# Loads that cast on their way into double-buffered bf16 tiles, in place of casts and spreads on Pool, and a last token tile in column halves

## The chip, the cores and the metric

One core of one Trainium2 chip. The metric is the device time of one execution in microseconds (us), taken as the median of several executions. A profile is one execution with every instruction recorded; its span is some 1.7 us shorter than the time of the same execution (325.9 for 327.63 in before). The engines are TensorE (PE, with its weight loads PEld), VectorE (DVE), ScalarE (ACT), Pool (POOL, GpSimd) and SyncE (SP). "L289" is a line of the kernel whose profile is shown; the changed kernel's lines are a few further down (L289 of before is L298 of after, 295 is 304, 411 is 420, 412 is 421, 454 is 463).

## The reference, cut to what matters

```python
def _attn_ref(q, k, v):                     # (8 batches, 8 heads, 576, 64), f32
    scores = matmul(q, k.T) / sqrt(64)
    mask_local   = (rel >= 0) & (rel < 32)                        # heads 0 to 3
    mask_strided = (rel >= 0) & (pos[None] % 32 == pos[:, None] % 32)   # heads 4 to 7
    attn = softmax(where(mask, scores, -1e9))
    return attn @ v

def _moe_ref(x, w_in, w_out):               # x (4608, 512), w_in (512, 2048), w_out (2048, 512)
    h = x @ w_in
    g = where(h > 0, h, exp(min(h, 0)) - 1) # ELU
    return g @ w_out
```

The two matrix products of the second part are most of TensorE's work. The attention of batches 3 to 7 is woven between them, one batch in about 33 us.

## The kernel before

q, k and v of the local heads are loaded in f32 for most batches, and cast by Pool into one bf16 tile each. Strided v (`vs`) is loaded in bf16 and *spread* by Pool, that is, copied into a tile that holds columns of ones between the heads, so that one matmul gives both the products and the sums of the softmax.

```python
    ql32 = const([RS, HG, NS * D], F32, "ql32")      # f32, one buffer each
    kl32 = const([LQ, 2, 2, LB, D], F32, "kl32")
    vl32 = const([128, 2, 2, LB, D], F32, "vl32")
    qlb = const([RP, 2, NS, 2 * D], BF16, "qlb")     # bf16, one buffer each
    klb = const([LQ, 2, LB, 2 * D], BF16, "klb")
    vlx = [const([128, 2, LB, 3 * D], BF16, f"vlx{i}") for i in range(2)]   # v, ones, v
    vsx = [const([RS, 2, NS, 3 * D], BF16, f"vsx{i}") for i in range(2)]
    # ... cut ...
    for b in range(3, B):                            # places in the schedule of batch b
        st = int(SC[b][0])
        ld, sp, ca, tr = (9, 3, 5, 3) if b == 3 else (9, 6, 5, 3)
        if b > 3:
            at(st - ld, lambda b=b: (load_str(b, qs, q), load_str(b, ks, k), load_str(b, vs, v),
                                     load_kl(b, nc.gpsimd), load_ql(b, nc.gpsimd),
                                     load_vl(b, nc.gpsimd)))
        at(st - sp, lambda b=b: spreads(b))          # 2 copies on Pool
        for i, f in enumerate(casts(b)):             # 2 casts each of k, q and v on Pool
            at(st - ca + .5 * i, f)
        at(st - tr, lambda b=b: Ts(b))               # 4 transposes by DMA
```

The mask multiplies and the ELU on VectorE:

```python
            nc.vector.tensor_mul(pm..., e..., mask_s...)          # L289, two SBUF inputs
            nc.vector.tensor_mul(pm, e, mb...)                    # L295, two SBUF inputs
    # ... cut; the ELU of one group of the first product ...
            eng.tensor_scalar(e1, e, scalar1=1.0, scalar2=1.0,    # L411, one SBUF input
                              op0=ALU.min, op1=ALU.subtract)
            nc.vector.tensor_tensor(gt, e1, hps, op=ALU.max)      # L412, hps is in PSUM
    # ... cut; the end of a tile of the second product ...
            nc.scalar.copy(o_sb, ops)                             # L459
            store(j * SUB + kk * 128, o_sb)
```

The softmax here doesn't subtract the row's maximum and nothing guards it: scores larger than these inputs give would overflow.

Of the kernel before, what the change touches and what calls it, by code (L numbers as in the profile page):

```python
# [17 lines left out]
D = 64  # L18
HG = 4
# [11 lines left out]
def kernel(  # L31
# [37 lines left out]

    ql32 = const([RS, HG, NS * D], F32, "ql32")  # L70
    kl32 = const([LQ, 2, 2, LB, D], F32, "kl32")
# [3 lines left out]
    vs = const([RS, HG, NS * D], BF16, "vs")  # L75
    qlb = const([RP, 2, NS, 2 * D], BF16, "qlb")
    qld = qlb.rearrange("p a s c -> p (a s c)").rearrange("p (h c) -> p h c", h=HG)
    klb = const([LQ, 2, LB, 2 * D], BF16, "klb")

    KLW = PRE + 2 * S  # L80
    KSW = 16 * RP + 48
# [30 lines left out]
    def load_ql16(b):  # L112
        nc.gpsimd.dma_start(out=qld[0:RS], in_=q[b, 0:HG].rearrange("h (p s) d -> p h (s d)", s=NS))

    def load_kl16(b):
        for h in range(HG):
            nc.gpsimd.dma_start(
                out=klb[:, h // 2, :, (h % 2) * D:(h % 2 + 1) * D],
                in_=k[b, h].rearrange("(t p) d -> p t d", p=LQ))

    def load_vl16(b):
        for h in range(HG):
# [3 lines left out]
            nc.gpsimd.dma_start(out=t[0:PRE, 1:], in_=x[LQ - PRE:, 0:LB - 1, :])  # L126

    def load_str(b, dst, src):
        nc.gpsimd.dma_start(  # L129
            out=dst[0:RS], in_=src[b, HG:2 * HG].rearrange("h (p s) d -> p h (s d)", s=NS))  # L130

    def cast_q(eng, a):
        o = qlb[0:RS, a].rearrange("p s (x d) -> p s x d", x=2)
        i = ql32[:, 2 * a:2 * a + 2].rearrange("p x (s d) -> p s x d", d=D)
        (eng.copy if eng is nc.scalar else eng.tensor_copy)(o, i)  # L135

    def cast_k(eng, a):
        (eng.copy if eng is nc.scalar else eng.tensor_copy)(  # L138
            klb[:, a].rearrange("p t (x d) -> p t x d", x=2),
            kl32[:, a].rearrange("p x t d -> p t x d"))  # L140
# [5 lines left out]

    def spread_v(eng, b, a):
        o = vsx[b % 2][:, a].rearrange("p s (y d) -> p s y d", d=D)[:, :, 0:3:2, :]
        i = vs[:, 2 * a:2 * a + 2].rearrange("p x (s d) -> p s x d", d=D)
        (eng.copy if eng is nc.scalar else eng.tensor_copy)(o, i)  # L150

    def dma_T(b, which):
        i = b % 2
        out_, in_, n = {
            "qs": (qsT[i], qs.rearrange("p h c -> p (h c)"), RP),
            "ks": (ksT[i][:, 0:16 * RP], ks.rearrange("p h c -> p (h c)"), RP),
            "ql": (qlT[i], qlb.rearrange("p a s c -> p (a s c)"), RP),
            "kl": (klT[i][:, PRE:], klb.rearrange("p a t c -> p (a t c)"), LQ),
        }[which]
        nc.sync.dma_start_transpose(out=out_.rearrange("p (c n) -> p c n", n=n), in_=in_)  # L160
# [30 lines left out]
    nc.gpsimd.iota(dist, pattern=[[1, RS]], base=RS, channel_multiplier=-1)  # L191
    nc.vector.memset(qlb[64:RP], 0.0)
    load_vl(0, nc.gpsimd)
# [33 lines left out]
    def t_parts(b, hp, nm):  # L227
# [5 lines left out]
        elif nm == "q":  # L233
            dst = qlT[i][:, a * 8 * n:(a + 1) * 8 * n]
            blk = ([qlb[0:n, a, j] for j in range(NS)] if b not in (1, 2) else
                   [[qld[0:n, 2 * a + x, j * D:(j + 1) * D] for x in range(2)]
                    for j in range(NS)])
        else:
            dst = klT[i][:, PRE + a * S:PRE + (a + 1) * S]
            blk = [klb[:, a, j] for j in range(LB)]  # L240
        return dst, blk
# [172 lines left out]
    def l1_wide(j, t):  # L414
# [5 lines left out]
        for mm in range(4):  # L420
            for c in range(KC):
# [4 lines left out]
                    start=(c == 0), stop=(c == KC - 1))  # L426
        e = p_wide.tile([128, 4, SUB], F32, tag="we", name="we")
        nc.scalar.activation(e, hps, ACT.Exp)
# [6 lines left out]

    def store(c0, o_sb):
        c = c0
        while c < c0 + 128:
            b, r = divmod(c, S)
            s, p = divmod(r, RS)  # L440
            n = min(RS - p, c0 + 128 - c)
            nc.sync.dma_start(out=out_v[b, s, p:p + n, :],
                              in_=o_sb[c - c0:c - c0 + n, :])
            c += n

    acc = {}

    def l2(j, kk, part, pool, tag):
# [8 lines left out]
        if part == 3:  # L457
            o_sb = p_wk.tile([128, d_model], F32, tag="osb", name="osb")
            nc.scalar.copy(o_sb, ops)  # L459
            store(j * SUB + kk * 128, o_sb)  # L460


# [70 lines left out]

    def casts(b):
        return ([lambda a=a: cast_k(nc.gpsimd, a) for a in range(2)]
                + [lambda a=a: cast_q(nc.gpsimd, a) for a in range(2)]
                + [lambda a=a: cast_v(nc.gpsimd, b, a) for a in range(2)])

    def spreads(b):
        for a in range(2):  # L540
            spread_v(nc.gpsimd, b, a)

    one_columns(1)
# [10 lines left out]
    load_wo(3)  # L554
    load_kl(1, nc.gpsimd)
    load_ql16(1)
    load_vl(1, nc.gpsimd)

# [8 lines left out]
    load_str(2, qs, q)  # L567
    load_str(2, ks, k)


# [3 lines left out]
    def l2_to(n):  # L574
        while l2n[0] < min(n, len(L2S)):
            j, kk, part = L2S[l2n[0]]
            late = kk and j == NSUB - 1
            l2(j, kk, part, *((p_h, "h") if late else (p_o, "o")))
            l2n[0] += 1

    for it in ("2 S4 2 S5 2 2 B4 S6 2 E4 A5 S7 2 E5 B6 a 2 E6 A7 2 E7 v "
               "T0 2 S0 S1 c 2 T1 k B0 2 E0 S2 2 A1 E1 S3 2 B2 E2 2 A3 2 E3 t 2 x").split():
        n = int(it[-1]) if it[-1].isdigit() else 0
        if it == "2":
            l2_to(l2n[0] + 1)
        elif it == "v":
            load_str(2, vs, v)
            load_vl16(2)
        elif it == "a":
            cast_k(nc.gpsimd, 0)  # L590
            for a in range(2):
                cast_v(nc.gpsimd, 1, a)
        elif it == "c":
            cast_k(nc.scalar, 1)
        elif it == "k":
            load_kl16(2)
            load_ql16(2)
            load_kl(3, nc.gpsimd)
            load_ql(3, nc.gpsimd)
            load_vl(3, nc.gpsimd)  # L600
        elif it == "t":
            for p in (2, 3):
                piece_T(2, p)
        elif it == "x":
            load_str(3, qs, q)
            load_str(3, ks, k)
        elif it[0] == "T":
            piece_T(1, n, (nc.vector, nc.scalar))
# [20 lines left out]
    for b in range(3, B):  # L629
        st = int(SC[b][0])  # L630
        ld, sp, ca, tr = (9, 3, 5, 3) if b == 3 else (9, 6, 5, 3)
        if b > 3:
            at(st - ld, lambda b=b: (load_str(b, qs, q), load_str(b, ks, k), load_str(b, vs, v),
                                     load_kl(b, nc.gpsimd), load_ql(b, nc.gpsimd),
                                     load_vl(b, nc.gpsimd)))
        at(st - sp, lambda b=b: spreads(b))
        for i, f in enumerate(casts(b)):
            at(st - ca + .5 * i, f)
        at(st - tr, lambda b=b: Ts(b))
    for b in range(2, B):  # L640
# [5 lines left out]

    at(SC[2][1] + 2, lambda: load_str(3, vs, v))
    L1S = [(j, t) for j in range(2, NSUB) for t in range(8)]
# [38 lines left out]
```

## Time and profile before

| | before |
|---|---|
| time before the change was run, median of 3 | 328.34 us (327.12 to 328.93) |
| profiled span | 325.9 us |
| last matmul ends | 4.1 us before the end |
| Pool's instructions that compute, per batch from 3 on | 8, about 8 us |

The prediction shows the page's shares and the stretches. Beside them I use two more views. The first is the page: its count of DMA packets, and groups of instructions (line, engine, operation, output and inputs, shapes, count, then busy us and mean ns of one, then idle time before them and what ended it).

```profile
DMA packets 55179, 41.98 MB, mean 129 GB/s; under 512 B 38296, under 2 KB 45784, under 8 KB 55144
...
L411 DVE TENSOR_SCALAR he<-he 128x512 bf16<-128x512 f32 x130 | 59.9, 461 | 20.5 <-ACT he L404 19.1
...
L295 DVE TENSOR_TENSOR pm<-e,mask_l 128x576 bf16<-128x576 bf16 x32 | 17.9, 591 | 3.3 <-ACT e L287 3.0
L150 POOL COPY vsx<-vs 72x1024 bf16<-72x1024 bf16 x10 | 11.2, 1146 | 23.9 <-DMA vs<-in_v_dram 18.8
```

The busy time of a group counts overlapping instructions once, so 17.9 us over 32 is 0.56 us each, a little under the mean of one.

The second view is TensorE's timeline (start in us, length of one, line, operation, tiles, shapes, count; in brackets the wait before it and what ended it).

```profile
31.25 1.03 PE L397 MATMUL hps<-xT,w_in_sb 128*128 128x256 bf16 x8 [0.39 <-DVE g L412]
...
120.45 0.30 PE L284 MATMUL sc<-qlT,klT 64*128 64x96 bf16 x6 [0.77 <-DVE xT L308]
...
218.85 0.30 PE L284 MATMUL sc<-qlT,klT 64*128 64x96 bf16 x6 [0.56 <-DVE xT L308]
```

The last two are gaps of the attention of batches 3 to 7: TensorE stands still while VectorE finishes.

### The profile page before, as it was taken

What the parts mean: (1) busy time and instruction counts of PE and PEld (TensorE: products, weight loads), DVE (VectorE), ACT (ScalarE), POOL (GpSimd) and SP (SyncE); (2) the same over time, 40 slices, a digit from 0 to 9 for tenths busy, and PEclk for the clock granted to TensorE, in tenths of its full rate; (3) what the DMA queues carried; (4) which work ended last, traced back from release to release, by engine and by line L of the source; (5) the groups of instructions that cost most, each with busy time, mean ns of one, the idle gap of its engine ahead of it and who ended that gap; (6) DMA issues with size and microseconds to landing.
All of it is one profiled execution on the core that took longest, in us unless ns stands there. A gap on an engine that the chain in (4) does not pass through costs nothing.

```text
span 325.9 us, 7664 instructions
## 1 busy us (share of the span) xinstructions
PE 309.4 (95%) x2933; PEld 222.6 (68%) x2976; DVE 246.0 (75%) x481; ACT 221.0 (68%) x429; POOL 101.2 (31%) x121
## 2 busy tenths in 40 slices
PE   8899997989999989999999999989999999999994
PEld 6669944566667767767777677757777777777762
DVE  6764973467778898898888988998888866666660
ACT  3798765687778877777778777877877734444431
POOL 6262414962672445263245443540000000000000
PEclk9999999999999999999999999999999999999999
DMA  8999999999799939992999299939111111111212
GB/s 165 192 207 209 221 185 151 141 193 184 114 126 214 202 87 146 224 183 68 132 224 217 70 144 232 174 92 162 48 45 37 34 34 32 33 34 44 55 32 64
DMA packets 55179, 41.98 MB, mean 129 GB/s; under 512 B 38296, under 2 KB 45784, under 8 KB 55144
## 3 DMA queue, kind: packets, MB, share of 16 engines
q0 software_dynamic: 21040, 24.49, 45.7%
q1 hardware_dynamic: 32780, 16.42, 24.6%
q10 hardware_dynamic: 1324, 0.59, 0.8%
q8 instruction: 23, 0.38, 0.5%
q14 instruction: 12, 0.10, 0.1%
HBM read 38.18 MB, written 9.44 MB: 146 GB/s over the span
## 4 chain that ended last, share of the span: by engine, by line
PE 74%; DVE 13%; ACT 5%; issue 4%; DMA 3%; POOL 0%; DVEq 0%; ACTq 0%
PE ops L454 32%; PE hps L397 30%; DVE g L412 3%; PE ox L336 3%; PE sc L284 3%; DVE he L411 3%; DMA ks<-in_k_dram 3%; DVE xT L304 2%; PE idle L464 1%; DVE pm L295 1%; DVE g L431 1%; PE hpw L422 1%; DVE xT L308 1%; PE tp L261 1%; PE o_ps L369 1%
## 5 line engine op out<-in xcount | busy, mean ns | idle before, releaser
L454 PE MATMUL ops<-w_out_sb,g 128*128 128x512 bf16 x533 | 140.5, 380 | 2.7 <-issue 0.8
L397 PE MATMUL hps<-xT,w_in_sb 128*128 128x256 bf16 x1088 | 140.7, 273 | 0.6 <-DVE g L412 0.4
L397 PEld LDWEIGHTS <-w_in_sb 128*128 128x128 bf16 x1088 | 117.4, 114 | 22.7 <-issue 0.6
L404 ACT ACTIVATE he<-hps 128x512 f32<-128x512 f32 x136 | 80.2, 593 | 53.7 <-PE hps L397 52.7
L412 DVE TENSOR_TENSOR g<-he,hps 128x512 bf16<-128x512 bf16 x130 | 89.4, 687 | 13.5
L454 PEld LDWEIGHTS <-g 128*128 128x128 bf16 x576 | 52.0, 98 | 39.1 <-DVE g L412 0.3
L411 DVE TENSOR_SCALAR he<-he 128x512 bf16<-128x512 f32 x130 | 59.9, 461 | 20.5 <-ACT he L404 19.1
L287 ACT ACTIVATE e<-sc 128x576 bf16<-128x576 f32 (+1 forms) x64 | 38.6, 645 | 4.5 <-PE sc L284 4.4
L459 ACT COPY osb<-ops 128x512 f32<-128x512 f32 x36 | 21.1, 587 | 15.5 <-PE ops L454 13.2
L339 ACT ACTIVATE ln<-ox 64x288 f32<-64x288 f32 x40 | 16.3, 409 | 12.3 <-PE ox L336 11.7
L304 DVE TENSOR_TENSOR xT<-ox,rc 64x288 bf16<-64x288 f32 x40 | 18.1, 453 | 5.0 <-ACT rc L342 4.7
L308 DVE TENSOR_TENSOR xT<-ox,rc 64x288 bf16<-64x288 f32 x40 | 18.1, 453 | 4.0 <-ACT rc L342 3.7
L295 DVE TENSOR_TENSOR pm<-e,mask_l 128x576 bf16<-128x576 bf16 x32 | 17.9, 591 | 3.3 <-ACT e L287 3.0
L150 POOL COPY vsx<-vs 72x1024 bf16<-72x1024 bf16 x10 | 11.2, 1146 | 23.9 <-DMA vs<-in_v_dram 18.8
L342 ACT ACTIVATE rc<-ln 128x288 f32<-128x288 f32 x40 | 17.7, 443 | 1.3
L289 DVE TENSOR_TENSOR pm<-e,mask_s 72x576 bf16<-72x576 bf16 x32 | 16.0, 527 | 2.5 <-ACT e L287 2.2
L340 ACT ACTIVATE ln<-ox 64x288 f32<-64x288 f32 x40 | 16.1, 402 | 0.5
L464 PE MATMUL idle<-warm 128*128 128x256 bf16 x92 | 15.1, 312 | 1.3 <-DVE warm L173 1.3
L144 POOL CAST vlx<-vl 128x768 bf16<-128x768 f32 x13 | 10.6, 843 | 17.6 <-DMA vl<-in_v_dram 16.6
L138 POOL CAST klb<-kl 96x768 bf16<-96x768 f32 x11 | 9.8, 907 | 19.9 <-DMA kl<-in_k_dram 14.8
L129 POOL DMA_DIRECT2D qs<-in_q_dram x8 | 6.5, 806 | 29.9 <-DMA qsT<-qs 25.2
L135 POOL CAST qlb<-ql 72x1024 bf16<-72x1024 f32 x10 | 11.6, 1186 | 3.8 <-DMA ql<-in_q_dram 3.8
(98 smaller groups left out, 256.4 us busy)
## 6 DMA issues: line engine op xcount, KB each, us to landing
out_dram<-osb SPq DMA_DIRECT2D x32, 144.0 KB
vl<-in_v_dram POOLq DMA_DIRECT2D x7, 576.0 KB, 17.8
kl<-in_k_dram POOLq DMA_DIRECT2D x6, 576.0 KB, 14.6
ql<-in_q_dram POOLq DMA_DIRECT2D x5, 576.0 KB, 15.7
qs<-in_q_dram POOLq DMA_DIRECT2D x8, 288.0 KB, 7.4
ks<-in_k_dram POOLq DMA_DIRECT2D x8, 288.0 KB, 9.7
vs<-in_v_dram POOLq DMA_DIRECT2D x8, 288.0 KB, 9.7
w_in_sb<-in_moe_w_in_dram POOLq DMA_DIRECT2D x2, 1024.0 KB, 16.3
```

The lines of the kernel that those rows point to most:

```text
L287: nc.scalar.activation(e[0:R], sc[0:R, :, 0:W], ACT.Exp, scale=scale)
L295: nc.vector.tensor_mul(pm, e, mb.unsqueeze(1).to_broadcast([128, 2, W]))
L304: nc.vector.tensor_mul(xs[:, u * W:(u + 1) * W], o[pr], rc[pr])
L308: nc.vector.tensor_mul(dst, o[pr].rearrange(pat, b=3, s=NS), rc[pr].rearrange(pat, b=3, s=NS))
L342: nc.scalar.activation(rc, ln, ACT.Exp, scale=-1.0)
L397: nc.tensor.matmul(hps[:, mm], lhsT=w_in_of(m, c), rhs=xT[:, c, r0:r0 + SUB], start=(c == 0), stop=(c == KC - 1))
L404: nc.scalar.activation(e, hps, ACT.Exp)
L411: eng.tensor_scalar(e1, e, scalar1=1.0, scalar2=1.0, op0=ALU.min, op1=ALU.subtract)
L412: nc.vector.tensor_tensor(gt, e1, hps, op=ALU.max)
L454: nc.tensor.matmul(ops, lhsT=g[:, m, kk * 128:(kk + 1) * 128], rhs=w_out_sb[:, m, :], start=(m == 0), stop=(m == MC - 1))
L459: nc.scalar.copy(o_sb, ops)
L464: nc.tensor.matmul(ps, lhsT=warm[:, 0:128], rhs=warm[:, 0:ps.shape[-1]], start=True, stop=True, skip_group_check=True)
```

## The change

The intent: let the loads cast, so that Pool computes nothing after the start and VectorE gets its shared memory port back. The targets need two buffers, since a load now writes straight into what the transposes read. (The space comes from one f32 tile, `big`, that batch 0's q and the wide exponentials of the start now share.) At the end, the last tile of the output is computed in two column halves, so that the first half is copied and stored while TensorE does the second.

```diff
-    qlb = const([RP, 2, NS, 2 * D], BF16, "qlb")
-    klb = const([LQ, 2, LB, 2 * D], BF16, "klb")
+    qlb = [const([RP, 2, NS, 2 * D], BF16, f"qlb{i}") for i in range(2)]
+    klb = [const([LQ, 2, LB, 2 * D], BF16, f"klb{i}") for i in range(2)]
+    def load_vsx16(b):                      # strided v, cast and spread by the load
+        for h in range(HG):
+            nc.gpsimd.dma_start(
+                out=vsx[b % 2][:, h // 2, :, 2 * (h % 2) * D:(2 * (h % 2) + 1) * D],
+                in_=v[b, HG + h].rearrange("(p s) d -> p s d", s=NS))
 ... (load_ql16 and load_kl16 alike, one load a head; cast and spread helpers go) ...
+    nc.vector.memset(qlb[1][64:RP], 0.0)
+    nc.vector.memset(vlx[1][0:PRE, :, 0, :], 0.0)
     one_columns(1)
 ...
-    load_kl(1, nc.gpsimd)
+    load_kl16(1)
     load_ql16(1)
-    load_vl(1, nc.gpsimd)
+    load_vl16(1)
 ... (batch 2's loads move up; ScalarE's cast of half of batch 1's k goes) ...
-            at(st - ld, lambda b=b: (load_str(b, qs, q), load_str(b, ks, k), load_str(b, vs, v),
-                                     load_kl(b, nc.gpsimd), load_ql(b, nc.gpsimd),
-                                     load_vl(b, nc.gpsimd)))
-        at(st - sp, lambda b=b: spreads(b))
-        for i, f in enumerate(casts(b)):
-            at(st - ca + .5 * i, f)
-        at(st - tr, lambda b=b: Ts(b))
+            at(st - 13, lambda b=b: (load_str(b, qs, q), load_str(b, ks, k), load_kl16(b),
+                                     load_ql16(b), load_vsx16(b), load_vl16(b)))
+        at(st - (3 if b == 3 else 4), lambda b=b: Ts(b))
 ... (the last tile) ...
+    def l2_last(j, kk):
+        g, n = g_of[j], d_model // 2
+        for i in range(2):
+            ... 16 matmuls of 128x256 into ops ...
+            nc.scalar.copy(o_sb[:, i * n:i * n + n // 2], ops[:, 0:n // 2])
+            nc.vector.tensor_copy(o_sb[:, i * n + n // 2:(i + 1) * n], ops[:, n // 2:])
+            store(..., slice(i * n, (i + 1) * n), (nc.sync, nc.scalar))
```

## The prediction

> **What bounds the kernel now.** I read the page's busy shares first, then the chain that ended last, then the busy time by stretches of 20 us, then TensorE's own timeline.
>
> ```profile
> PE 309.4 (95%) x2933; PEld 222.6 (68%) x2976; DVE 246.0 (75%) x481; ACT 221.0 (68%) x429; POOL 101.2 (31%) x121
> ...
> PE 74%; DVE 13%; ACT 5%; issue 4%; DMA 3%; POOL 0%; DVEq 0%; ACTq 0%
> ```
>
> TensorE is busy 309.4 of 325.9 us and makes up three quarters of the chain. Pool, whose casts the change removes, is 0% of the chain: nothing that ended last waited directly for Pool for long. So at most the 16.5 us in which TensorE idles can be won, and the question is where those lie. The stretches (columns: length, then busy us and count of PE, PEld, DVE, ACT, POOL, then clock, DMA share, GB/s) say:
>
> ```profile
> 0.00:20.00 20.00, 17.36 (x227) 12.58 (x227) 13.80 (x40) 12.39 (x22) 9.24 (x17) 1.00 1.02 182
> ...
> 40.00:60.00 20.00, 17.64 (x207) 8.94 (x210) 10.28 (x22) 13.27 (x28) 8.03 (x12) 1.00 1.08 167
> 60.00:80.00 20.00, 18.16 (x231) 13.17 (x231) 14.06 (x29) 14.57 (x30) 11.52 (x15) 1.00 1.22 177
> ...
> 200.00:220.00 20.00, 18.70 (x177) 13.26 (x178) 18.84 (x34) 15.39 (x31) 8.33 (x8) 1.00 0.76 156
> ...
> 240.00:260.00 20.00, 19.84 (x174) 14.76 (x175) 17.40 (x37) 15.46 (x32) 0.00 (x0) 1.00 0.13 38
> ```
>
> From 240 us on, where Pool has stopped and the DMA engines are nearly empty, TensorE idles 0.16 us in 20: that is the floor. The six stretches of 100 to 220 us (batches 3 to 7 in attention) leave 0.53, 0.91, 0.17, 0.39, 0.38 and 1.30 us idle, 3.7 in all, 2.7 above the floor. The stretches from 40 to 80 us (batches 1 and 2) leave 2.4 and 1.8. The rest is the start (2.6 in the first 20 us, before any changed code) and the end (after the last matmul about 4 us).
>
> What causes the 2.7 us? In TensorE's timeline the gaps of batches 3 to 7 name VectorE, and VectorE's instructions just before them are slow. Here is one gap, and the mask multiply of line 289 in two stretches (length, then busy and count, clock, DMA share, GB/s): first while Pool only issues loads, then while it spreads v.
>
> ```profile
> 139.64 0.42 PE L336 MATMUL ox<-pm,vsx 72*128 72x72 bf16 x8 [0.30 <-DVE pm L289]
> ```
>
> ```profile
> 127.30:132.00 4.70, 0.82 (x2) 1.00 1.08 140
> ...
> 138.20:140.50 2.30, 2.17 (x2) 1.00 0.99 134
> ```
>
> So 0.41 us each becomes 1.09 us each as soon as Pool computes. The local mask multiply (line 295) does the same: 0.41 us without Pool, 1.03 us from 178.7 to 181.0 us while Pool casts q. The ELU's tensor_scalar (line 411) is 0.425 us from 226 to 256 us, with no Pool work, against a mean of 0.461, and single ones reach 0.88 and 1.19 us in the chain (at 209.2 and 115.4 us). The ELU's max (line 412), which reads PSUM, is 0.69 us everywhere.
>
> **What the Trainium skill says.** "SBUF — State Buffer", section "Who interferes with whom": VectorE and GpSimd share one SBUF port pair under an exclusive lock held for the whole instruction. VectorE's two-port modes (tensor_scalar can enter one) and its instructions with two SBUF inputs are blocked by a Pool instruction that reads SBUF; those with at most one SBUF input outside those modes are not. The trace agrees exactly: lines 289, 295 (two SBUF inputs) and 411 stretch, line 412 (one SBUF, one PSUM input) does not. "DMA: Bandwidth & Descriptors", section "SWDGE vs HWDGE vs iDMA": a cast during a DMA needs a DMA issued from GpSimd. The trace agrees in that every casting load here sits on Pool's queue, and the stretch above shows VectorE at its fast 0.41 us while Pool issues them. The same page, "Why small descriptors are slow (HBM only)": each packet and descriptor carries a fixed overhead. The trace supports it roughly: batch 2's cast loads in 128-byte runs are the densest in packets (4,632 in 10 us from 54 to 64 us).
>
> **The change, part by part.**
>
> (1) Casts and spreads leave Pool. Per batch from 3 on Pool did 2 casts each of k (0.83 us), q (1.2) and v (0.83) and 2 spreads (1.1), about 8 us of computing. VectorE gets back: line 411, 59.9 us minus 130 x 0.425 = 4.6 us; line 295, 17.9 minus 32 x 0.41 = 4.8; line 289, 16.0 minus 13.1 = 2.9. That is 12 us of VectorE time over the run. Most of it lies beside a busy TensorE. What reaches the end is the 2.7 us above the floor (the five named gaps of this stage alone add up to 0.77 + 0.30 + 0.32 + 0.58 + 0.56 = 2.5). I count **-2.7 us**.
>
> (2) Batch 1's k cast leaves ScalarE as well. TensorE waited for it:
>
> ```profile
> 56.00 0.43 PE L261 MATMUL tp<-identity,klb 96*128 96x96 bf16 x6 [0.52 <-ACT klb L138]
> ```
>
> In the chain that cast took 0.72 us. I count **-0.5 us**. The 1.3 us gap at 53.7 us (klT copied by ScalarE behind batch 1's normalization) has another cause and stays.
>
> (3) Loads. The bytes read from HBM are the same; q and v of the later batches go in 256-byte pieces instead of 2 KB ones. Pool issues 22 loads a batch instead of 7. From the cast loads of batch 2, one issue is 0.6 to 0.78 us, so about 16 us a batch, against 8 of computing plus some 7 of issuing before: Pool stays near 100 us busy, now all issue. Pieces per batch rise from about 6,200 (2,304 k, 3,040 v, 288 each for the other three and q) to about 10,500. From 55.5 to 64 us Pool issued about 5,300 such pieces, which landed 3 to 6 us after their issue, so in some 10 us, so a batch needs about 20 us of DMA (an estimate). A batch has 33 us (transposes issue at 87.0, 120.1, 153.9 us), of which the transposes take some 8. It fits. The loads of a batch begin when the previous batch's transpose of qs has landed, and k and q come before v, so they land 10 us or so before the next transposes. I count **0 us** for batches 4 to 7.
>
> Batches 2 and 3 are tighter, as DMA is saturated up to 80 us. The strided v of batch 2 now stands behind batch 2's k, q and v in Pool's order. Before, it was issued at 54.75 us and landed 5.2 us later; now, at the 220 GB/s of reads that 57 to 85 us sustained (6.2 MB), it lands at about 68 to 71 us. TensorE first multiplies with it at 70.0 us. Likewise qs and ks of batch 3 landed at 85 to 86 us, its transposes were issued from 87.0, and its first scores ran at 95.5; now v of batch 3 is still loading beside those transposes. Each may cost 0 to 2 us, and TensorE idled 0.37 + 1.16 us for VectorE right at the first place, which a wait there would cover. I count **+0.8 us**.
>
> (4) The last tile in halves:
>
> ```profile
> 321.85 0.59 ACT L459 COPY osb<-ops 128x512 f32<-128x512 f32 x1 [2.87 <-PE ops L454]
> ```
>
> The matmuls stream the same columns (128x512 at 0.216 us, 128x256 at 0.109). After the last one the 0.59 us copy becomes two copies of a quarter tile side by side, perhaps 0.3 us, and the last stores (issued from 322.4 to 323.2 us on one queue) are half as large on two queues. I count **-0.6 us**; the remaining 2.7 us to landing stay.
>
> (5) Added: two memsets on VectorE near 23 us (about 0.9 us like that of qs, while VectorE waits for the first wide exponential at 26.5 us): 0.
>
> Sum: -2.7 - 0.5 + 0.8 - 0.6 = -3.0 us on 328.3: about 325.3.
>
> **The rivals.**
> *A. Pool's work was hidden, so nothing moves.* For it: Pool is 0% of the chain and VectorE only 13%. Against it: the gaps follow Pool's computing and vanish after 220 us. It would give 327 to 328 us (the tail alone).
> *B. A late load takes the place of the cast.* Cast loads in small pieces, eight outstanding at most (in the built program each waits for the eighth before it), arrive late for batch 2's strided v or batch 3's transposes. For it: the DMA share is about 1 from 0 to 80 us. Against it: the same bytes, no pause any more while Pool waits for v (5.8 us before 53.2 us), and buffers that are double. It would cost 2 to 5 us: 327 to 330.
> *C. The lock costs more than its gaps*, since VectorE's delays also hold PSUM and shift ScalarE and TensorE groups slightly (the ox groups after a gap took 0.42 us instead of 0.26). All of TensorE's excess in 36 to 220 us then goes: another 2 us, 323.
>
> **Range and chances.** A gives the upper side, C the lower, B the tail above. Predicted 325.2 us, with 322.6 to 328.2 to hold it 8 times in 10. 2% is 6.6 us; to win that, nearly every removable gap would have to go, as start and end hold 6 of the 16.5 idle us. To lose it needs a DMA-bound stage of several microseconds in each batch. Faster 0.04, same 0.93, slower 0.03.
>
> **What would show it.** Right: VectorE near 234 us instead of 246, lines 289 and 295 at 0.41 us each, TensorE's idle time from 100 to 220 us at about 1 us, Pool's busy time only load issues. A wait of TensorE on the DMA of vs near 70 us, or on the transposes near 95 us, would show B, and how large. If lines 289 and 295 are fast and TensorE's idle time stays, step 1 is wrong. If Pool's issues stretch well past 0.75 us, or the DMA share stays at 1 through each batch, step 3 is wrong.

## The result, and the profile after

| | before | after |
|---|---|---|
| median | 328.63 us (327.12 to 329.01, 4 runs) | 324.71 us (324.33 to 325.27, 4 runs) |
| profiled span | 325.9 us | 322.6 us |
| Pool busy | 101.2 us | 115.6 us |
| read from HBM | 38.18 MB | 38.04 MB |

The ratio is 0.9891, with a 95% interval of 0.9854 to 0.9927. A ratio here and below is the mean time of one kernel's fast runs over the mean of the other's fast runs of the same rounds, so it is not quite the ratio of the medians. Executions over 1.5% slower than the fastest of the same kernel are left out of the means. By the 2% rule this is "same": about 3.9 us faster by the medians, predicted 3.0. The total lies within half a microsecond of the prediction, but its terms do not; the rest of the document is about them.

The page of the changed kernel, the lines that answer to those of before:

```profile
PE 310.8 (96%) x2992; PEld 223.6 (69%) x2992; DVE 239.5 (74%) x485; ACT 220.2 (68%) x429; POOL 115.6 (36%) x162
...
DMA packets 113990, 36.36 MB, mean 113 GB/s; under 512 B 101154, under 2 KB 107458, under 8 KB 113954
...
PE 83%; DVE 6%; ACT 5%; DMA 3%; issue 1%; SPq 0%; DVEq 0%; ACTq 0%
...
L420 DVE TENSOR_SCALAR he<-he 128x512 bf16<-128x512 f32 x130 | 57.7, 444 | 20.9 <-ACT he L413 19.5
...
L304 DVE TENSOR_TENSOR pm<-e,mask_l 128x576 bf16<-128x576 bf16 x32 | 13.5, 453 | 3.3 <-ACT e L296 3.0
```

VectorE's part of the chain fell from 13% to 6%. The local mask multiply went from 17.9 to 13.5 us, which is 0.42 us each. The tensor_scalar gained only 2.2 us. The packets doubled, and the DMA share of the chain is 3% in both. Nearly half of it is new, though: 4.38 us from 186.96 us on are a DMA transpose of `ks`, for which TensorE then waits 0.14 us.

Busy time by stretches (length, then busy us and count of PE, PEld, DVE, ACT, POOL, then clock, DMA share, GB/s):

```profile
0.00:20.00 20.00, 16.52 (x224) 11.85 (x224) 13.84 (x39) 12.12 (x21) 8.72 (x16) 1.00 1.02 180
...
40.00:60.00 20.00, 18.52 (x217) 9.79 (x216) 11.37 (x24) 13.18 (x26) 14.40 (x21) 1.00 1.48 157
60.00:80.00 20.00, 18.82 (x239) 13.30 (x238) 13.48 (x30) 15.24 (x32) 16.90 (x23) 1.00 1.45 134
...
200.00:220.00 20.00, 20.00 (x185) 14.56 (x184) 17.65 (x35) 15.49 (x33) 9.35 (x13) 1.00 1.22 125
```

TensorE is busy 20.00 us of the 20 from 200 to 220 us, where before it was 18.70. Such numbers need care. This trace has all 560 full-width matmuls of the second product (and the 32 half-width ones of the last tile), that of before only 533 of 576, and a missing matmul looks like idle time. So the "floor" of 0.16 us in the prediction was missing records: from 240 to 260 us, 37 such matmuls are recorded for 41 weight loads, and the idle time lies in four gaps of about 0.05 us in front of such matmuls. I therefore located the gain in another way: I took the start of the same matmul in both traces and watched where the difference changes. Missing records do not disturb this, and I call it "by position" below.

| between (time in before) | after minus before goes from, to | step | what lies there |
|---|---|---|---|
| start to 20.5 us | 0 to +0.31 | +0.31 | first loads land; this varied from -0.5 to +1.1 between runs of unchanged code |
| to 31.25 us | to +1.24 | +0.93 | the second half of the first wide groups |
| to 56.00 us | to +0.67 | -0.57 | transposes of batch 1's k |
| to 86.39 us | to +0.21 | -0.46 | batch 2 |
| to 218.85 us | to -3.27 | -3.48 | attention of batches 3 to 7, in steps of 0.2 to 1.0 at the gaps |
| last matmul's end | 321.81 to 318.57 | -3.24 in all | |
| from there to the end | 4.12 to 4.04 | -0.07 | last copies and stores |

TensorE's timeline of after at the places shown of before:

```profile
32.49 1.03 PE L406 MATMUL hps<-xT,w_in_sb 128*128 128x256 bf16 x8 [1.32 <-DVE g L421]
...
56.67 0.43 PE L270 MATMUL tp<-identity,klb 96*128 96x96 bf16 x6
...
119.54 0.43 PE L293 MATMUL sc<-qlT,klT 64*128 64x96 bf16 x12
...
215.44 0.43 PE L293 MATMUL sc<-qlT,klT 64*128 64x96 bf16 x12
```

The gaps at 120.45 and 218.85 us are gone: where before two groups of 6 stood around a wait, 12 matmuls now run in one piece. But at 32.49 us a wait of 0.39 has become one of 1.32 us. The engines' timelines before it show why (start, length, engine):

```profile
25.15 0.91 DVE L557 MEMSET qlb<- 16x1024 uint32 x1 [0.27 <-issue]
...
26.15 0.22 DVE L558 MEMSET vlx<- 32x192 uint32 x1
...
26.40 0.83 ACT L528 COPY vlx<-warm 128x768 bf16<-128x768 bf16 x1 [2.01 <-DVE vlx L558]
...
28.09 1.02 ACT L437 ACTIVATE big<-hpw 128x1024 f32<-128x1024 f32 x1
```

ScalarE's copy of the columns of ones writes the same tile as VectorE's second memset, so it waits 2.01 us for it, and the first wide exponential, queued behind that copy, starts at 28.09 us. In before it started at 26.52. A memset of 16 partitions cost 0.91 us, not on a busy engine, but in front of another engine's queue.

### The profile page after: what moved, and what is told of

It is laid out like the page before. It is cut to its first block, busy times and chain, and to the rows that moved or that the text cites. A ratio compares the mean times of both kernels' runs of the same rounds, so it can differ in the third digit from the quotient of the medians.

```text
span 322.6 us, 7819 instructions
## 1 busy us (share of the span) xinstructions
PE 310.8 (96%) x2992; PEld 223.6 (69%) x2992; DVE 239.5 (74%) x485; ACT 220.2 (68%) x429; POOL 115.6 (36%) x162
## 2 busy tenths in 40 slices
DMA packets 113990, 36.36 MB, mean 113 GB/s; under 512 B 101154, under 2 KB 107458, under 8 KB 113954
## 3 DMA queue, kind: packets, MB, share of 16 engines
HBM read 38.04 MB, written 9.44 MB: 147 GB/s over the span
## 4 chain that ended last, share of the span: by engine, by line
PE 83%; DVE 6%; ACT 5%; DMA 3%; issue 1%; SPq 0%; DVEq 0%; ACTq 0%
PE ops L463 36%; PE hps L406 33%; PE sc L293 4%; PE ox L345 3%; DVE g L421 2%; DMA kl<-in_k_dram 2%; DMA ksT<-ks 1%; PE idle L487 1%; DVE g L440 1%; PE opl L478 1%; PE tp L270 1%; DVE he L420 1%; ACT vsx L528 1%; ACT big L437 1%; ACT e L296 1%
## 5 line engine op out<-in xcount | busy, mean ns | idle before, releaser
L463 PE MATMUL ops<-w_out_sb,g 128*128 128x512 bf16 x560 | 143.6, 380 | 0.1
L463 PEld LDWEIGHTS <-g 128*128 128x128 bf16 x560 | 50.4, 98 | 37.2 <-DVE g L421 0.3
L420 DVE TENSOR_SCALAR he<-he 128x512 bf16<-128x512 f32 x130 | 57.7, 444 | 20.9 <-ACT he L413 19.5
L468 ACT COPY osb<-ops 128x512 f32<-128x512 f32 x35 | 20.5, 587 | 12.3 <-PE ops L463 9.4
L125 POOL DMA_DIRECT2D klb<-in_k_dram x28 | 20.7, 747 | 7.9 <-DMA w_in_sb<-in_moe_w_in_dram 5.2
L133 POOL DMA_DIRECT2D vlx<-in_v_dram x28 | 21.9, 782 | 4.1 <-DMA w_out_sb<-in_moe_w_out_dram 1.9
L119 POOL DMA_DIRECT2D qlb<-in_q_dram x20 | 16.6, 833 | 13.8 <-DMA ks<-in_k_dram 10.0
L134 POOL DMA_DIRECT2D vlx<-in_v_dram x28 | 17.3, 618 | 4.2 <-DMA qlb<-in_q_dram 2.1
L138 POOL DMA_DIRECT2D vsx<-in_v_dram x20 | 16.2, 816 | 0.9 <-DMA klb<-in_k_dram 0.9
L304 DVE TENSOR_TENSOR pm<-e,mask_l 128x576 bf16<-128x576 bf16 x32 | 13.5, 453 | 3.3 <-ACT e L296 3.0
L487 PE MATMUL idle<-warm 128*128 128x256 bf16 x92 | 14.3, 299 | 1.3 <-DVE warm L182 1.3
```

Of the source, the lines that this page charges most:

```text
L125: nc.gpsimd.dma_start(out=klb[b % 2][:, h // 2, :, (h % 2) * D:(h % 2 + 1) * D], in_=k[b, h].rearrange("(t p) d -> p t d", p=LQ))
L133: nc.gpsimd.dma_start(out=t[PRE:128], in_=x)
L420: eng.tensor_scalar(e1, e, scalar1=1.0, scalar2=1.0, op0=ALU.min, op1=ALU.subtract)
L463: nc.tensor.matmul(ops, lhsT=g[:, m, kk * 128:(kk + 1) * 128], rhs=w_out_sb[:, m, :], start=(m == 0), stop=(m == MC - 1))
```

## The experiments

Twelve experiments ran, in three calls, each on another chip; each call had its own runs of the kernel before (medians 328.25, 327.62 and 328.53 us, 11 runs each), so runs of different calls are compared by their ratios or by position. By the 2% rule run 5 and run 9 are slower, run 11 is "unclear" (its interval holds 2%), and all others are the same as before.

| run | median us | range, runs | ratio to before | 95% interval |
|---|---|---|---|---|
| after | 324.71 | 324.33 to 325.27, 4 | 0.9891 | 0.9854 to 0.9927 |
| 1 memsets on Pool | 323.81 | 322.34 to 324.48, 6 | 0.9861 | 0.9813 to 0.9909 |
| 2 last tile whole | 324.72 | 323.69 to 325.09, 6 | 0.9886 | 0.9844 to 0.9928 |
| 3 useless copies | 328.60 | 327.71 to 329.73, 4 | 1.0010 | 0.9955 to 1.0065 |
| 4 useless memsets | 326.68 | 326.24 to 327.51, 4 | 0.9953 | 0.9901 to 1.0005 |
| 5 v alone, wrong order | 359.17 | 356.75 to 360.75, 4 | 1.0950 | 1.0899 to 1.1002 |
| 6 transposes later | 325.21 | 324.24 to 327.38, 6 | 0.9927 | 0.9891 to 0.9963 |
| 7 k cast on ScalarE | 325.46 | 324.46 to 326.63, 6 | 0.9926 | 0.9892 to 0.9960 |
| 8 halves, one copy each | 324.48 | 324.08 to 326.22, 6 | 0.9905 | 0.9875 to 0.9935 |
| 9 v alone | 340.20 | 337.58 to 341.95, 5 | 1.0339 | 1.0282 to 1.0396 |
| 10 after again | 324.49 | 323.76 to 325.06, 6 | 0.9866 | 0.9824 to 0.9908 |
| 11 the best parts | 324.02 | 322.94 to 325.60, 6 | 0.9843 | 0.9796 to 0.9890 |
| 12 twice the copies | 329.43 | 329.19 to 332.71, 4 | 1.0041 | 0.9979 to 1.0102 |

**The theory**: Pool's computing slowed VectorE through the port they share, and TensorE waited; the load issues that took its place do not. **The rivals**: that the gain comes from elsewhere (batch 1's k, the tail, or the earlier transposes), and, within the theory, that any Pool work counts or only the kind that reads memory. Runs 3, 4 and 12 put useless Pool work back; 9 takes half of it away; 1, 2, 6, 7 and 8 change the small parts singly.

### 1. The two memsets on Pool, beside the weight loads

```diff
+    nc.gpsimd.memset(qlb[1][64:RP], 0.0)          # after the w_in loads
+    nc.gpsimd.memset(vlx[1][0:PRE, :, 0, :], 0.0)
 ...
-    nc.vector.memset(qlb[1][64:RP], 0.0)          # ahead of one_columns(1)
-    nc.vector.memset(vlx[1][0:PRE, :, 0, :], 0.0)
     one_columns(1)
```

> The changed kernel, but its two new memsets (0.91 and 0.22 us on VectorE, which ScalarE waited 2.0 us for before it could start the first wide exponential) are done by Pool while Pool waits for the first v load. Theory: the memsets cost TensorE 0.93 us at the second half of the first wide group (its gap of 1.32 us there against 0.39 before). Then this run is 0.9 us faster than the changed kernel: about 0.986 of the kernel before (changed: 0.989), span about 321.7. Rival: the first stage waits for the w_in load or the exponentials anyway and the gap comes back later: same time as the changed kernel, span 322.6.

By position the matmul at 32.49 us of after came 1.27 us sooner, so the whole added wait went, and 0.8 to 1.05 us were still there later (0.88 at the last matmul's end). On Pool the memsets take 1.8 and 0.4 us and nobody waits for them. This shows the +0.93 us step of the table. The medians agree in sign, 323.81 against 324.72 of run 2, which is after but for its tail, in the same rounds, though the intervals of the two overlap.

### 2. The last tile as before

```diff
-            if (j, kk) != (NSUB - 1, 1):
-                l2(j, kk, part, p_o, "o")
-            elif part == 0:
-                l2_last(j, kk)
+            late = kk and j == NSUB - 1
+            l2(j, kk, part, *((p_h, "h") if late else (p_o, "o")))
```

> The changed kernel with the last token tile as before: one full-width accumulation, one copy by ScalarE, stores on one queue. Theory: the halves bring nothing, because VectorE's half copy waits for ScalarE's (0.27 + 0.29 us one after the other against 0.59) and the rest is the landing: same as the changed kernel within 0.2 us, from the last matmul's end to the end of the span 4.0 to 4.1 us in both. Rival (my prediction's step 4): the halves bring 0.6 us, so this run is 0.6 us slower than the changed kernel.

The time does not move, and the end comes 4.10 us after the last matmul, against 4.04. The tails of after and of this run (start, length, engine; the copies after the last matmul and, of after, the first store):

```profile
318.61 0.27 ACT L481 COPY osb<-opl 128x128 f32<-128x128 f32 x1 [1.48 <-PE opl L478]
...
318.91 0.29 DVE L482 COPY osb<-opl 128x128 f32<-128x128 f32 x1 [1.46 <-ACT osb L481]
...
319.23 0.34 ACTq L451 DMA_DIRECT2D out_dram<-osb  x1
```

```profile
318.62 0.59 ACT L468 COPY osb<-ops 128x512 f32<-128x512 f32 x1 [2.87 <-PE ops L463]
```

The two quarter copies do not run side by side. VectorE's starts when ScalarE's has ended, and the profile names that copy as what it waited for. In the built program one waits for the other because they use the same tiles; whether the shared PSUM tile or the shared output tile is what orders them no run separates. "PSUM — Partial Sum Buffer", section "PSUM bank collisions raise a hardware error", of the Trainium skill gives a reason why they must not overlap in any case: two engines on one PSUM bank and the same partitions at once are an error, even when both only read, and the two quarters lie in one 128x256 f32 tile, 1 KB a partition. No run here shows such an error, as the program kept them apart. Serially they take until 319.20 us, 0.59 us after the first began, which is exactly the length of the whole copy.

### 8. Halves with one copy each

```diff
-            nc.scalar.copy(o_sb[:, i * n:i * n + n // 2], ops[:, 0:n // 2])
-            nc.vector.tensor_copy(o_sb[:, i * n + n // 2:(i + 1) * n], ops[:, n // 2:])
+            nc.scalar.copy(o_sb[:, i * n:(i + 1) * n], ops)
```

> The changed kernel with each half of the last tile copied by ScalarE alone in one instruction of 128x256 instead of two quarter copies that wait for each other. Theory: the last copy takes about 0.38 us (between 0.27 for 128 columns and 0.59 for 512) instead of 0.59 in two steps: 0.2 us faster than the changed kernel, from the last matmul's end to the end of the span about 3.8 us. Rival: the landing of the last stores sets the end whatever the copy does: no change.

```profile
319.01 0.37 ACT L481 COPY osb<-opl 128x256 f32<-128x256 f32 x1 [1.37 <-PE opl L478]
```

One copy of a half takes 0.37 us, less than two quarters in turn (0.59), and the end comes 3.79 us after the last matmul instead of 4.04. That is 0.25 us in one profile; in the times (324.48 us, against 324.71 and 324.49 of after) it cannot be seen.

### 7. Half of batch 1's k cast by ScalarE again

```diff
-    load_kl16(1)
+    for h in range(2):                            # heads 0 and 1 as in the change
+        nc.gpsimd.dma_start(out=klb[1][:, 0, :, h * D:(h + 1) * D], in_=k[1, h]...)
+    load_kl(1, nc.gpsimd, 1)                      # heads 2 and 3 in f32
 ...
-               "T0 2 S0 S1 2 T1 k ..."
+               "T0 2 S0 S1 c 2 T1 k ..."          # c: cast_k(nc.scalar, 1) into klb[1]
```

> The changed kernel, but the second half of batch 1's local k is loaded in float32 and cast by ScalarE as in the kernel before. Theory: TensorE's gap of 0.52 us before the second transposes of batch 1 comes back: 0.5 to 0.6 us slower than the changed kernel. Rival: the gap is taken up by the later gap on VectorE near 70 us: no change.

By position the loss comes back where it was won: +0.59 us at the transposes of batch 1's k (57.20 us instead of 56.67), and it stays to the end. The profile of this run also has a short stretch of half TensorE clock at 57 to 61 us, which costs about 1.4 us and need not belong to the change; the median is 1 us above that of run 8 in the same rounds, and the intervals overlap.

### 6. The transposes one place later

```diff
-        at(st - (3 if b == 3 else 4), lambda b=b: Ts(b))
+        at(st - 3, lambda b=b: Ts(b))
```

> The changed kernel with the DMA transposes of batches 4 to 7 issued three units ahead of use, as in the kernel before, instead of four. Theory (only Pool's computing mattered): same as the changed kernel within 0.3 us. Rival (the earlier transposes took a wait away): 0.5 to 2 us slower than the changed kernel, with gaps of TensorE on the transposes at the start of each batch.

From 74 to 219 us the matmuls keep their place against those of after within 0.4 us, and are 0.1 us later at the end of it. But the edit did not do what it was meant to. SyncE issues the transposes in order with the stores, which wait for ScalarE's copies of the output (75.7 us in all from 80 to 230 us), and they went out at the same place as in after. The first transpose of batch 4, in after and in this run:

```profile
120.28 1.57 SPq L169 DMA_TRANSPOSE qsT<-qs  x1
```

```profile
123.26 1.58 SPq L169 DMA_TRANSPOSE qsT<-qs  x1
```

It is 2.98 us later in a run whose TensorE is 2.95 us later there, and the other batches are alike. So run 6 tests nothing. The rival that the gain of 3.5 us came from earlier transposes falls all the same, by the first two traces: from before to after the first transposes of batches 4 to 7 moved by +0.17, -1.56, -1.93 and -2.54 us, and TensorE's matmuls there by +0.17, -1.59, -1.92 and -2.54. In TensorE's program they were not earlier at all. The run's profile is 3.1 us longer than that of after for two other reasons: a start that was 1.1 us late, and this:

```profile
72.00:74.00 2.00, 0.71 (x15) 0.56 (x12) 1.90 (x5) 1.51 (x5) 2.00 (x3) 0.92 2.19 128
74.00:76.00 2.00, 2.00 (x17) 1.18 (x16) 0.71 (x2) 1.02 (x3) 2.00 (x4) 0.50 1.78 105
```

The columns are those of the stretches above, in steps of 2 us. The clock (the third number from the end) falls to 0.50 right after 2 us in which TensorE was busy for only 0.71. "TensorE: Matmul & The Clock Gate", section "What's actually happening", of the Trainium skill says that a block watches how busy TensorE has been and halves its clock after an idle window of about 3.4 us. The trace agrees on the half clock and on what precedes it, not on the length: TensorE was idle for less than 2 us in one piece here, and the two matmul-rich microseconds before (70 to 72) were 1.85 busy. The stretches of runs 6 and 7 cost about 1.4 us each. They fell in some profiles (runs 6, 7, 9, 11) and not in others of nearly the same code.

### 3 and 4. Useless Pool work put back: copies, or memsets

Both add eight instructions per batch from batch 3 on, at about the place of the old casts, in sizes like theirs. They write a part of a tile that nothing uses at that time. The copies read old data, the memsets read nothing.

```diff
+    scr = big[:, 1024:2048].bitcast(BF16)[:, 0:1024]
+    def dummy(b, write_only):
+        for src, shape in 2 * ((kl32, (96, 768)), (big, (72, 1024)), (vl32, (128, 768)), (vs, (72, 1024))):
+            o = scr[0:shape[0], 0:shape[1]]
+            nc.gpsimd.memset(o, 0.0) if write_only else nc.gpsimd.tensor_copy(o, src)
 ...
+        at(st - 6, lambda b=b: dummy(b, write_only))
```

> The changed kernel, plus eight useless copies on Pool per batch from batch 3 on, of the sizes of the casts and spreads of before (float32 or bf16 read from SBUF, bf16 written, results never used). Loads, buffers and the transposes' place stay as in the changed kernel. Theory (the port that VectorE and Pool share): lines 298 and 304 (mask multiplies) rise from 0.45 us towards 0.55 mean, the gaps of TensorE between 86 and 219 us come back, and 2 to 3.5 us are lost: about 326 us, ratio near 0.997. Rival (the earlier transposes and the double buffers brought it): no change, 324.7 us.

> As the run with useless copies on Pool, but the eight instructions per batch are memsets: they write the same areas and read nothing. Theory by the Trainium skill's section on who interferes with whom: an instruction with two SBUF inputs (mask multiplies) only meets Pool's reads and keeps its 0.41 us, the tensor_scalar in a two-port mode meets any Pool instruction. So TensorE loses little, under 1 us against the changed kernel. Rival: any Pool computing slows VectorE alike, mask multiplies too, and 2 to 3.5 us are lost as with the copies.

The copies take the whole gain back: 328.60 us, the time of before. By position, they cost 3.5 us from 72 to 223 us (from +1.50 to +4.99 against after), the same size as the -3.48 us step. This shows the cause of that step: take Pool's computing away and TensorE gains, put useless computing of the same kind back, with loads and double buffers left as in after, and the gain is gone. That the sizes agree so closely is luck in part. The copies come eight in a row and not at the places of the old casts, and the strided mask multiply (L298) kept its 13.5 us, where I had expected it to rise with L304. Late loads are no rival: of the five waits of TensorE over 0.2 us from 74 us on, four end with VectorE. The fifth, 0.68 us at 163 us, ends with the transpose of `ks`; after itself, in run 10, waits 0.35 us there.

The memsets cost 3.0 us by position, where I had expected under 1; in the medians it is 2.0 us (326.68 against 324.72 of run 2 in the same rounds, where the copies cost 3.9). The two views, first of the copies, then of the memsets (the group of the ELU's tensor_scalar and of the local mask multiply):

```profile
L420 DVE TENSOR_SCALAR he<-he 128x512 bf16<-128x512 f32 x130 | 62.1, 478 | 20.7 <-ACT he L413 19.3
...
L304 DVE TENSOR_TENSOR pm<-e,mask_l 128x576 bf16<-128x576 bf16 x32 | 17.2, 566 | 3.3 <-ACT e L296 2.8
```

```profile
L420 DVE TENSOR_SCALAR he<-he 128x512 bf16<-128x512 f32 x130 | 62.9, 484 | 20.6 <-ACT he L413 19.2
...
L304 DVE TENSOR_TENSOR pm<-e,mask_l 128x576 bf16<-128x576 bf16 x32 | 13.5, 452 | 3.3 <-ACT e L296 2.8
```

Copies slow both groups; memsets slow the tensor_scalar as much (62.9 us against 57.7 in after) and leave the mask multiply at exactly its 13.5 us. This is what "SBUF — State Buffer", section "Who interferes with whom", says: an instruction with two memory inputs meets only a Pool instruction that reads, one in a two-port mode meets any. What I got wrong was which of the two matters for the end. The tensor_scalar is the only group of VectorE that differs from after by more than 0.2 us, and 2 to 3 us were lost, so slower tensor_scalars alone can cost more than half of what the copies cost.

### 12. Twice as many copies

```diff
-        for src, shape in 2 * (...):
+        for src, shape in 4 * (...):
```

> The run with useless Pool copies, twice as many (sixteen per batch from batch 3 on). With eight it lost 3.5 us between 86 and 223 us against the changed kernel. Theory (time of Pool computing sets what TensorE loses): about twice that, 6 to 8 us, a time near 331 to 332 us. Rival (only the coincidence with a batch's turn costs, and VectorE catches up afterwards): clearly less than twice, under 5 us.

The loss by position from 72 to 231 us is 4.3 us, against 3.5 with eight copies. It is not in proportion: the second eight cost 0.8. So how long Pool computes in all does not set the loss. That it counts whether a copy meets a VectorE instruction that TensorE is about to wait for fits this; no run moves the copies to test it.

### 5 and 9. The kernel before, with v alone cast by the loads

The kernel before with `load_vsx16` and `load_vl16` for batches 3 to 7 and without spreads and casts of v. Pool keeps four casts a batch (k, k, q, q), half of its computing.

```diff
-            at(st - ld, lambda b=b: (..., load_str(b, vs, v), ..., load_vl(b, nc.gpsimd)))
-        at(st - sp, lambda b=b: spreads(b))
+            at(st - ld, lambda b=b: (..., load_vsx16(b), ..., load_vl16(b)))
 ...                                  # casts(b): k and q only; batch 3 alike
```

> The kernel before with one part of the change alone: from batch 3 on, v (local and strided) is cast by the loads straight into the tiles that hold it, so Pool loses its two spreads and two v casts a batch (about 3.9 of 7.9 us of computing) and keeps the casts of k and q. Transposes, their place and the single buffers of q and k stay. Theory (shared port): roughly half of TensorE's 3.5 us of gaps between 86 and 219 us go: 1 to 2.5 us faster than the kernel before, ratio 0.993 to 0.997. Rival (the gain needs the double buffers and the earlier transposes): same as before within 0.5 us.

> The corrected one-part kernel (in the first try the load of batch 3's local v stood before batch 1's last use of the same buffer, so it gave a wrong result and TensorE waited 19.9 us for it; the load now stands behind those uses). The kernel before, with v of batches 3 to 7 cast by the loads, k and q still cast by Pool. Theory (Pool's computing slows VectorE): 1 to 2.5 us faster than the kernel before, ratio 0.992 to 0.997; by program position, TensorE gains roughly half of the changed kernel's 3.5 us between 86 and 219 us. Rival (the double buffers or the earlier transposes of q and k are needed): no gain.

Run 5 was a mistake of mine: batch 3's load into one buffer of `vlx` stood ahead of batch 1's last use of that buffer. It gives a wrong result (relative error 0.2), and TensorE waited 19.88 us for that load. Nothing follows from its time. In run 9 the load stands after that use, and the result is right.

Run 9 was to be 1 to 2.5 us faster than before, as half of Pool's computing goes. It was 3.4% slower, 340.20 us. By position it loses 8.4 us from 86 to 219 us, of which about 1.5 fall in a stretch of half clock (at 189 us of this run). The timelines of VectorE and Pool at one of the places (start, length, instruction), and TensorE's after another of them:

```profile
151.37 4.15 DVE L417 TENSOR_SCALAR he<-he 128x512 bf16<-128x512 f32 x1
```

```profile
151.68 1.60 POOL L144 CAST klb<-kl 96x768 bf16<-96x768 f32 x2
...
153.22 2.02 POOL L141 CAST qlb<-ql 72x1024 bf16<-72x1024 f32 x2
```

```profile
119.62 0.42 PE L342 MATMUL ox<-pm,vlx 128*128 128x96 bf16 x6 [3.30 <-DVE pm L301]
```

One tensor_scalar that takes 0.43 us elsewhere took 4.15: it ended only when Pool's four casts, from 151.68 to 155.24 us without a pause, were done. The same happened at 115 us (two mask multiplies, 4.62 us) and 184 us (a tensor_scalar, 3.53 us); TensorE's wait of 3.30 us shown is the one after 115. In the kernel before, the casts waited in pairs for their data (Pool waited 1.29 us for q in the middle of such a run at 114 us), and the two mask multiplies caught there took 1.66 us together, the tensor_scalar after them 1.25. So less work on Pool cost more, and the trace shows where: one VectorE instruction waited for four casts. Why it did not get the port between two of them stays open. That they came in one piece is not enough to explain it. In the kernel before, two casts of q follow each other without a pause from 113.90 to 116.32 us, and the mask multiply caught there is done 0.31 us after the first has ended. In runs 3 and 12, eight and sixteen copies follow each other with 0.06 us between them, and no VectorE instruction beside them takes more than 1.29 us, about one copy (of run 3, least, median and longest time in ns):

```profile
L304 DVE TENSOR_TENSOR pm<-e,mask_l x32: 447/452/1294, 10.5 to 254.7; 128x576 bf16<-128x576 bf16 x32
```

No run puts a pause between the casts of run 9.

### 10 and 11. After again, and the best parts together

Run 11 is after with the memsets of run 1, the tail of run 8, and, on my guess, both copies of one transposed pair of batch 1 on VectorE: `piece_T(1, n)` in place of `piece_T(1, n, (nc.vector, nc.scalar))`.

> The changed kernel itself once more, beside its variants on one chip: about 0.989 of the kernel before. Its profile also shows how far the start (landing of the first loads) and short drops of the clock move the span by themselves, by up to about 1 us each in the runs so far.

> The changed kernel with three mends: the two new memsets on Pool while it waits for the first v load (measured 0.9 us), each half of the last tile copied by ScalarE in one instruction (0.2 us), and both copies of batch 1's local transposes on VectorE, as ScalarE's copy had to wait for VectorE's of the same PSUM tile (TensorE's gap of 1.30 us there should shrink to about 1.0). Theory: the parts add up to 1.3 to 1.5 us: about 323.3 us where the changed kernel has 324.7, ratio near 0.985. Rival: the gains of the first stage are lost again at the gap of 1.05 us near 72 us, leaving under 0.6 us.

After repeated itself within 0.3 us at every position from 46 us on (0.45 us earlier at 10 us). Run 11 has a lower median than both kernels (324.02 against 324.49 and 328.53 us), and its ratio over that of after in the same rounds is 0.9843/0.9866 = 0.9977, some 0.7 us. That is about half of what I expected, and it lies well inside the intervals, so run 11 beats the kernel before clearly (whether by 2% is unclear) and after not for certain. Its profile holds a stretch of half clock from about 16 to 26 us, so the positions in it tell little.

## Why the prediction was right or wrong, point by point

- **The total** (325.2 predicted, 324.71 measured) and the class were right. The terms were -2.7, -0.5, +0.8, -0.6 and 0; by position they are -3.5, -0.6, 0, -0.07 and +0.9, with +0.3 of jitter at the start and -0.5 in batch 2. Errors of both signs cancelled, so that the sum came so close was luck.
- **(1) Casts and spreads off Pool: right in mechanism, too small.** Run 3 shows it by putting the loss back. The term was sized by the idle time of TensorE. By position the five named gaps gave 3.1 us, not 2.5, and two more places (at 145 and 186 us, where before shows hardly any idle time) 0.6; a wait for a transpose took 0.2 back at 193 us. Rival C (all of the excess) came nearer: from 36 to 219 us 4.5 us went in all. On VectorE's side, the mask multiplies did reach their fast case (two of them take 0.81 us in the stretch below, shown for L298 while Pool issues loads). The tensor_scalar did not: it won 2.2 us, not 4.6.

```profile
127.30:133.00 5.70, 0.81 (x2) 1.00 1.36 156
```

  The step that failed there is the silent one that load issues cost VectorE nothing because L289 stayed fast beside them. L289 is no witness for the tensor_scalar: in run 4 Pool's memsets also left the mask multiplies alone and slowed the tensor_scalar. The tensor_scalar in after (length, busy and count, clock, DMA share, GB/s) took 2.67/5 = 0.53 us where Pool is busy issuing for 8.72 of 10 us, and 2.13/5 = 0.43 where it is busy for 0.04:

```profile
170.00:180.00 10.00, 2.67 (x5) 1.00 1.77 151
180.00:190.00 10.00, 2.13 (x5) 1.00 0.41 83
```

  One by one it is clearer. Of the tensor_scalars of after from 60 us on, 84 run beside no load issue, and none of them takes more than 0.43 us; 38 overlap one, and 14 of these take more than 0.46, up to 0.71. Run 10 repeats it (none of 85, and 13 of 37). So only those beside a load issue are slow, if not all of them; no run takes the issues away. VectorE as a whole stood at 239.5 us and not near 234, since the two memsets (1.13 us) and the tail's copies (0.58) were not counted either.
- **(2) Batch 1's k off ScalarE: right**, -0.57 us by position, and run 7 brings back 0.59.
- **(3) Loads: the +0.8 us for batches 2 and 3 did not come**, and neither did rival B. The timeline of Pool shows it: the load of batch 2's strided v was issued at 61.04 us and had landed by 68.59, where the next load, which waited for its place, starts. TensorE uses it first at 70.45 us.

```profile
61.04 0.74 POOL L143 DMA_DIRECT2D vs<-in_v_dram  x1 [0.16 <-issue]
...
68.59 0.90 POOL L119 DMA_DIRECT2D qlb<-in_q_dram  x1 [1.35 <-DMA vs<-in_v_dram]
...
124.67 0.74 POOL L143 DMA_DIRECT2D qs<-in_q_dram  x1 [11.31 <-DMA qsT<-qs]
```

  So the margin was 1.9 us, inside the 68 to 71 us I had worked out; the term was a hedge on a date, and the date held. In later batches Pool waits 11.31 us with nothing to issue until a transpose has freed `qs`, as the last line shows: there is slack, as predicted. Pool's busy time rose to 115.6 us, not about 100; no wait of a matmul over 0.1 us from 84 us on names Pool. Other parts of this step were off without costing much. By the prediction's own counts the kernel before has 6,496 pieces a batch, not about 6,200, and the packets on Pool's queue rose far more than pieces were to, from 21,040 to 79,696. The DMA share from 86 to 220 us went from 0.88 to 1.18, though it falls low once in every batch; "stays at 1" had been my sign of an error here. And TensorE's matmuls now wait a little for the transpose of `ks`, which they did not in before: 0.14 us at 191 us, in run 10 0.35 us at 159 and again at 191 us. Why that transpose lands later no run shows. Last, that batch 2's loads were dense in packets is a count and supports no cost per packet.
- **(4) The tail: wrong.** The step "two copies of a quarter tile side by side, perhaps 0.3 us" failed: they run one after the other, 0.27 and 0.29 us. I had not asked what orders two copies that share a PSUM tile and an output tile. The stores being half as large on two queues did not shorten the rest. Runs 2 and 8 show it.
- **(5) The memsets: wrong.** "While VectorE waits" was true of VectorE. It left out who else writes that tile: ScalarE waited 2.01 us for the memset, and 0.93 us of it reached the end. Run 1 shows it.
- **What stays open**: the jitter of the first 20 us, which moves single runs by about a microsecond; the short half-clock stretches; and whether run 11 or run 1 is the better kernel.

## What to carry to other kernels

When Pool and VectorE overlap, ask of each VectorE instruction how it uses the shared port, and look in the trace at how long single ones wait: here mostly for one Pool instruction (up to 1.29 us), in run 9 for four (4.15 us). Check after an edit that the instruction it moves did move: run 6's transposes had not. A helper instruction placed in an engine's idle time is free only if no other engine's queue stands behind the tile that it writes. Check a total by its parts: compare when the same matmul starts in both traces, since errors of opposite sign can give the right sum.

## What the Trainium skill lacked or had wrong

- "SBUF — State Buffer", section "Who interferes with whom", says that who issues first has the shared pair "for the whole instruction". The runs show more than one instruction's wait: a tensor_scalar of 0.43 us took 4.15 us through four back-to-back Pool casts (run 9), while beside eight or sixteen copies in a row none took more than 1.29 us (runs 3 and 12). The page does not say who gets the port between two of them.
- The same section is right that Pool instructions that only write do not slow those with two SBUF inputs (13.5 us in run 4, as in after), and that a two-port instruction meets them (57.7 to 62.9 us). It gives no hint which costs more: here the write-only work still cost 3.0 us by position where copies cost 3.5 (2.0 and 3.9 in the medians).
- The same section speaks of VectorE starving Pool's load issues. What the issues cost VectorE it does not say: of the tensor_scalars in after, none of the 84 beside no issue took more than 0.43 us, and 14 of the 38 beside one took 0.46 to 0.71 (coincidence in time, not isolated by a run).
- "DMA: Bandwidth & Descriptors", section "Why small descriptors are slow (HBM only)", gives the fixed cost per packet. Here the packets doubled from 55,179 to 113,990 at the same bytes read, and no wait of a matmul for a load or transpose from 84 us on was longer than 0.14 us (0.35 in run 10); the page does not say how to tell when that cost is hidden.
- "TensorE: Matmul & The Clock Gate", section "What's actually happening", ties the half clock to an idle window of about 3.4 us. In run 6 it came after 2 us with 0.71 us of matmuls, for a loss of about 1.4 us, in single executions only.
- The pages on reading profiles, "Perfetto Trace Analysis" and "NEFF Inspection", do not warn that matmul records can be missing from one profile and not from another (43 of 576 of the second product in before, none in after), which looks like idle time of TensorE.
